# A planned single-core kernel: verdict ordered early, its branch hinted, transpositions in float32r, a corrected cost table

## The chip, the cores and the metric

The kernel runs on one core of a Trainium2 chip. The metric is device time in microseconds (us) from start to end of one execution; the figure for a kernel is the median of several executions. The engines are called as in the profile: PE (matmuls) and PEld (its weight loads), DVE (vector), ACT (scalar), POOL (GpSimd), SP (which issues all DMAs here). PEldq, DVEq, ACTq, POOLq and SPq are their sequencers, which run branches, semaphore instructions and register loads.

## The reference

A gated linear recurrence ("attention") over 768 steps for 4 x 8 heads of 48, and then two feed-forward stages on 3072 tokens of 384:

```python
scale = np.minimum(mag, 0.999) / (mag + 1e-06)        # mag = |a|
for t in range(S):
    new_re = ar * S_re - ai * S_im                    # a = scaled (a_re, a_im) at t
    new_im = ar * S_im + ai * S_re
    S_re, S_im = new_re + outer(k[t], v[t]), new_im
    y[t] = q[t] @ S_re
h = x @ w_in                                          # 3072 x 384 @ 384 x 2048
x = softplus(h) @ w_out                               # back to 384
out = (((x @ w1) * (x @ w2)) @ w3) @ w_out2           # 1024 wide
```

The weights come as float64 bit patterns, two int32 words for a number.

## The kernel before, in words

**Attention.** The time axis is cut into 24 units of 128 steps (six for each of four batches). For unit `u`, `norm(u)` makes the scaled decay `a` (`s1` to `s4`: squares, a norm, a reciprocal root in logarithms on ACT, products on DVE), `scan` multiplies the decays up over two units at a time (DVE alone), `inv(u)` divides: `s3` and `s5` write q times P and k over P into the tile `qkp`, real and imaginary part, and `s6` sends `qkp` to DRAM (`pd`) and reads it back by heads into `rs`. `mm(u)` then transposes the k half of `qkp` on PE (`kt(0)`, `kt(1)`: three transpositions each, copied to `kT` by ACT), forms the scores from `rs` (`sc`), masks them on DVE (`am`), and forms the output `yp` and the new state (`stp`). The last unit of a batch needs no state and so no transposition; units 0 and 1 take a shortcut without DRAM (`pick`).

**First feed-forward** (blocks "A"): nine blocks of tokens. `s1` multiplies with `w_in`, softplus runs on ACT and DVE, `s2a` multiplies with `w_out`. The first two blocks are in float32; the other seven split each operand into a high and a low float32r part and use three products. They run beside the attention of later tokens.

**Second feed-forward** (blocks "B"): six blocks of 512 tokens, `s3` (two products `pa`, `pb`, multiplied on DVE, split on ACT and DVE) and `s2b` with w3 and w_out2, which `early()` has multiplied together at the start (`wpa`).

**Verdict.** The fast path holds for ordinary inputs only. `check` collects minima and maxima of all weights (80 pieces, during blocks B), and at the end of the program comparisons are drawn together to one number `oki` in SBUF: DVE reduces to one column `okp`, PE transposes it to a row `okt`, DVE reduces that to `oki`. Each engine loads `oki` into a register (`values_load`) and compares; if the verdict is 0 a slow path, `general`, runs. It stands in the program between the branch and the end, so with a verdict of 1 every engine jumps over it.

**What sets the order.** All instructions of the fast path are recorded by `Plan.add` with a cost from the table `Plan.cost` and their dependencies. `Plan.flush` lays them out on the engines by list scheduling, back and forth, 16 rounds with one fixed seed, takes the best by its own costs, and emits them in that order; each engine then runs its own queue in order. The costs set nothing but the order. Nearly every instruction is issued from one line of `Plan.add` (L211 in the profile), so instructions are told apart by their tiles. Tiles with the same tag share buffers (`qkp` has one buffer; `n2` has one), and an instruction that writes a buffer waits for the readers of the tile that was there.

```python
order = sorted((k for k in start if self.ops[k][0]), key=lambda k: (start[k], k))
with self.tc.manual_schedule():
    for k in order:
        for call in self.ops[k][1]:
            call()
```

Of the kernel before, what the change touches and what calls it, by code (L numbers as in the profile page):

```python
# [66 lines left out]

VH = 64
# [11 lines left out]
class Plan:  # L80
# [57 lines left out]
    def cost(self, eng, op, outs, ins):  # L138
        n = max(self.free_size(x) for x in (*outs, *ins))
        if eng == "SP":  # L140
            size = 2 if outs[0].dtype == I16 else 4
            for _, n in outs[0].ap:
                size *= n
            rate = 270 if hasattr(ins[0].tensor, "tag_meta") else RATE
            cost = max(650 if n < 512 and self.on_chip(ins[0]) else 475, size / rate)
            if not self.on_chip(outs[0]):
                land = 5200
            elif self.on_chip(ins[0]):
                land = 2300
            elif hasattr(ins[0].tensor, "tag_meta"):  # L150
                land = 6800
            else:
                land = 2500 + size / rate
            return cost, max(land - cost, 0)
        if eng == "PE":
            n = self.free_size(outs[0])
            if op == "transpose":
                return 109, 250
# [3 lines left out]
            return ((0.75 * n + 24) / (2 if m <= 32 else 1) if m <= 64 else max(n, m) / 0.6 + 5), 250  # L162
# [3 lines left out]
        if eng == "ACT":  # L166
            return 105 + 0.88 * n, 200
# [155 lines left out]
    def flush(self):  # L323
# [26 lines left out]
        with self.tc.manual_schedule():  # L350
            for k in order:
                for call in self.ops[k][1]:
                    call()
# [13 lines left out]
def fused(ctx: ExitStack, tc: tile.TileContext, a_in, qk_in, v_in, wio, w12, w3t, wo2, q, k, v, a_re, a_im, outT):  # L367
# [38 lines left out]
    nc.vector.tensor_scalar(out=mask, in0=mask, scalar1=whenf, scalar2=None, op0=ALU.is_ge)  # L406
# [3 lines left out]
    nc.gpsimd.memset(eps_p, 1e-18)  # L410
    m2max = cp.tile([P, NCH], F32, name="m2max")
# [57 lines left out]
    def norm(u):  # L469
# [20 lines left out]
        def s3():  # L490
# [3 lines left out]
            A.activation(out=gt(n[:, 1]), in_=w, func=AF.Copy, scale=5e-7, bias=1.0)  # L494
            A.activation(out=gt(n[:, 0]), in_=w, func=AF.Copy, scale=-0.4995)

        def s4():
            n = s["nt"]
            V.scalar_tensor_tensor(
                out=n[:, 0], in0=n[:, 0], scalar=1.0, in1=n[:, 1], op0=ALU.min, op1=ALU.mult  # L500
# [131 lines left out]
    def inv(u):  # L632
# [55 lines left out]

        if u < PICK:
            return [s1, s2, s3, lambda: pick(0), s4, s5, lambda: pick(1)]  # L690
        return [s1, s2, s3, s4, s5, s6]

    def mm(u):
# [142 lines left out]
    wtop = [wp.tile([P, 2 * DM], I32, tag=tag, name=f"wtop_{tag}") for tag in ("ws", f"wa{FA - 1}")]  # L836
    for x in wtop:
        GP.memset(x, 0)

# [278 lines left out]
    for i, n in enumerate(("min", "max")):  # L1118
        bst[n] = lims[:, i * NCK : (i + 1) * NCK]
    b_x(0)  # L1120
    it = 0
    nit = (NBB - 1) * FB
    for bi in range(NBB):
        gq = {}
        for f in range(FB):
# [13 lines left out]
    for i, n in enumerate(("min", "max")):  # L1139
        V.tensor_reduce(  # L1140
            out=wlim[:, i : i + 1], in_=bst[n], axis=mybir.AxisListType.X, op=getattr(ALU, n)
        )
    okp = ap.tile([P, DM], F32, tag="v", bufs=VB, name="okp")
    c0 = 0
    for src, lim, op in (
        (pend.rearrange("p b g -> p (b g)"), 1e-3, ALU.is_ge),
        (m2max, 1e15, ALU.is_le),
        (wlim[:, 0:1], 2.0**-28, ALU.is_ge),
        (wlim[:, 1:2], 2.0**32, ALU.is_lt),
    ):  # L1150
        n = src.shape[1]
        V.tensor_scalar(out=okp[:, c0 : c0 + n], in0=src, scalar1=lim, scalar2=None, op0=op)
        c0 += n
    ok1 = okp[:, DM - 1 : DM]
    V.tensor_reduce(out=ok1, in_=okp[:, 0:c0], axis=mybir.AxisListType.X, op=ALU.min)
    okt = pst("s1", S1B, [P, NB], "okt")[0:1, 0:P]
    PE.transpose(okt, ok1, ident)
    V.tensor_reduce(out=oki, in_=okt, axis=mybir.AxisListType.X, op=ALU.min)
# [245 lines left out]
```

## Time and profile before

| | |
|---|---|
| median of 3 executions | 920.21 us (919.09 to 921.62) |
| the profiled execution, its own time | 920.99 us |
| its span, first to last instruction | 919.1 us |
| PE busy | 883.7 us, 96% of the span |
| DVE, ACT, POOL busy | 706.2, 517.2, 9.9 us |
| granted TensorE clock, mean | 0.996 of full speed |
| DMA moved | 139.16 MB, 151 GB/s |

PE's busy time joins overlapping matmuls, whose ends are modelled: it shows where PE had something to do, and not how fast. How fast is read from pieces of the chain of waits, where a run of n like matmuls stands with its length. Times inside the span count from its start. The 1.9 us between the span and the execution's own time lie outside it.

### The profile page before, as it was taken

To read this page: it belongs to the slowest core of one execution; us is meant where nothing else is said; L and a number is where in the kernel's file an instruction comes from. 1 tells how busy PE (TensorE), PEld (TensorE's weight loads), DVE (VectorE), ACT (ScalarE), POOL (GpSimd) and SP (SyncE) were. 2 spreads that over 40 slices of the span, in tenths; PEclk is the share of its full clock that TensorE was granted. 3 is DMA by queue.
4 is the path that set the end of the run, shared out by engine and by line. 5 is a ranking of instruction groups with operands and counts; after the bars stand their busy time and mean duration, and the time that the engine had idled before them with its cause. 6 is when DMAs were issued, how large, how long until landed. Compare 5 with 4: busy or idle time off the path is not lost.

```text
span 919.1 us, 18336 instructions
## 1 busy us (share of the span) xinstructions
PE 883.7 (96%) x7177; PEld 794.3 (86%) x7177; DVE 706.2 (77%) x1739; ACT 517.2 (56%) x1056; POOL 9.9 (1%) x31
## 2 busy tenths in 40 slices
PE   3998899999999999999999999999999999999995
PEld 2577788898999999999999999998888888888884
DVE  6999999999999999898997563689878885232211
ACT  6688985777678685767775655772222222131212
POOL 4000000000000000000000000000000000000000
PEclk9999999999999999999999999999999999999998
DMA  9898736445465644544454361357788773000001
GB/s 338 315 369 309 183 114 143 130 118 137 121 177 139 170 109 121 142 116 132 124 133 124 98 165 63 104 147 245 239 275 244 260 230 109 0 35 1 35 1 39
DMA packets 81361, 139.16 MB, mean 151 GB/s; under 512 B 5872, under 2 KB 49776, under 8 KB 81264
## 3 DMA queue, kind: packets, MB, share of 16 engines
q1 hardware_dynamic: 81264, 137.89, 50.3%
q8 instruction: 58, 0.95, 0.5%
q14 instruction: 39, 0.32, 0.1%
HBM read 109.56 MB, written 28.31 MB: 150 GB/s over the span
## 4 chain that ended last, share of the span: by engine, by line
PE 78%; DVE 9%; DMA 6%; ACT 2%; issue 2%; SPq 1%; ACTq 0%; DVEq 0%
PE acc L211 29%; PE s L211 18%; PE pb L211 11%; PE pa L211 11%; PE yp L211 3%; PE sc L211 3%; DMA a<-a_in 3%; DVE P L211 2%; PE wpa L211 2%; DMA wr<-wio 2%; DVE tm L211 2%; SPq L211 1%; PE stp L211 1%; PE ktp L211 1%; DMA wpd<-wpe 1%
## 5 line engine op out<-in xcount | busy, mean ns | idle before, releaser
L211 ACT ACTIVATE e<-e 128x384 f32<-128x384 f32 (+2 forms) x288 | 134.5, 486 | 2.9
L211 DVE TENSOR_TENSOR bg<-pa,bg 128x512 f32<-128x512 f32 x48 | 33.1, 691 | 97.4 <-PE pa L211 81.8
L211 DVE TENSOR_TENSOR tm<-P 128x768 f32<-128x768 f32 (+4 forms) x240 | 101.0, 438 | 1.2
L211 ACT ACTIVATE e<-s 128x384 f32<-128x384 f32 (+2 forms) x144 | 64.9, 452 | 60.4 <-PE s L211 59.2
L211 DVE SCALAR_TENSOR_TENSOR e<-s,e 128x384 f32<-128x384 f32 (+2 forms) x144 | 72.6, 508 | 23.9 <-ACT e L211 23.6
L211 ACT CAST bgg<-bg 128x512 fp32r<-128x512 f32 x48 | 29.8, 621 | 98.1 <-DVE bg L211 98.1
L211 ACT COPY bg<-pb 128x512 f32<-128x512 f32 x48 | 28.2, 588 | 96.8 <-PE pb L211 84.3
L211 DVE TENSOR_TENSOR P<-tm 128x96 f32<-128x96 f32 (+9 forms) x328 | 76.2, 271 | 1.6
L211 ACT CAST gh<-e 128x384 fp32r<-128x384 f32 x112 | 56.8, 509 | 21.9 <-DVE e L211 21.8
L211 DVE TENSOR_TENSOR gl<-e,gh 128x384 fp32r<-128x384 f32 x112 | 61.7, 552 | 9.3 <-ACT gh L211 8.8
L211 PE MATMUL wpa<-wo,w 128*128 128x384 f32 x128 | 44.5, 505 | 14.1 <-DVE w L211 14.1
L211 PE MATMUL sc<-rs 112*128 112x128 f32 x384 | 53.6, 275 | 1.1 <-DVE e L211 1.1
L211 PEld LDWEIGHTS sc<-rs 112*128 112x128 f32 x384 | 51.6, 191 | 2.3 <-DVE e L211 1.5
L211 PEld LDWEIGHTS wpa<-wo,w 128*128 128x128 f32 x128 | 24.8, 198 | 30.8 <-DVE w L211 14.3
L211 PE MATMUL acc<-bgg,bwp0h 128*128 128x512 f32 x144 | 50.8, 389 | 0.0
L211 DVE CUSTOM_DVE_ANT_0 ck<-ckr 128x384 f32<-128x384 f32 x80 | 43.4, 543 | 9.2 <-DMA ckr<-wio 3.1
L211 PE MATMUL acc<-bgg,bwp2h 128*128 128x512 f32 x144 | 49.0, 389 | 0.0
L211 DVE TENSOR_TENSOR bgg<-bg,bgg 128x512 fp32r<-128x512 f32 x48 | 33.0, 688 | 15.7 <-ACT bgg L211 15.7
L211 DVE TENSOR_REDUCE lims<-ck 128x1 f32<-128x384 f32 x80 | 43.1, 538 | 2.3
L211 PE MATMUL s<-x,w 128*128 128x128 f32 (+1 forms) x192 | 38.0, 332 | 3.0 <-DVE E L211 0.9
L211 DVE TENSOR_TENSOR am<-sc,mask 128x512 f32<-128x512 f32 x48 | 32.9, 686 | 7.9 <-PE sc L211 7.8
L211 PE MATMUL acc<-e,w 128*128 128x128 f32 (+1 forms) x192 | 37.4, 329 | 1.1 <-issue 1.1
(385 smaller groups left out, 2325.0 us busy)
## 6 DMA issues: line engine op xcount, KB each, us to landing
pd<-qkp SPq DMA_DIRECT2D x22, 768.0 KB, 3.9
rs<-pd SPq DMA_DIRECT2D x44, 384.0 KB, 6.2
ckr<-wio SPq DMA_DIRECT2D x32, 384.0 KB, 3.7
wr<-wio SPq DMA_DIRECT2D x32, 383.8 KB, 6.9
a<-a_in SPq DMA_DIRECT2D x24, 384.0 KB, 4.8
qk<-qk_in SPq DMA_DIRECT2D x24, 384.0 KB, 3.4
v<-v_in SPq DMA_DIRECT2D x24, 256.0 KB, 4.4
w12r<-w SPq DMA_DIRECT2D x16, 384.0 KB, 3.4
```

Source lines behind the costliest of these rows:

```text
L211: getattr(engine.unit, op)(*args, **kw)
```

## The change

1. **Verdict early.** The comparisons, the transposition `okt` and the reduction `oki` are recorded when the fifth block B has been recorded, not after the sixth, with a dummy operation of 30000 behind them, so that the planner sees them as a chain of 30 us that must end in time. The register load loses its run-time bounds check.
2. **Hint.** The emitted program is cut at a third of the planned time. There each of PE, ACT, DVE and SP gets one instruction more, a branch prefetch hint that names the branch over `general`. POOL gets none.
3. **Transpositions.** Units 2 to 22 but the last of a batch (18 units) copy the k half of `qkp` by a DMA (SBUF to SBUF, 384 KB) into a float32r tile `kx`, which takes the buffer of `n2`. Their transpositions (6 for a unit, 108 in all) read `kx` in float32r with a float32r identity, which ACT copies once.
4. **Norm.** The second of two ACT copies in `s3` goes (24 in all); DVE's instruction in `s4` takes its place with other constants.
5. **Mask and fills.** The comparison that makes the mask goes from DVE to POOL; two fills of POOL come earlier.
6. **Cost table.** Float32r transpositions, narrow matmuls, DMAs within SBUF and ACT on bfloat16 get other costs. So the whole order is planned anew.

```diff
@@ cost
-                land = 2300
+                land = 2200 + size / rate
...
-                return 109, 250
+                return (82 if ins[0].dtype == F32R else 109), 250
...
-            return ((0.75 * n + 24) / (2 if m <= 32 else 1) if m <= 64 else max(n, m) / 0.6 + 5), 250
+            return ((0.75 * n + 8) / 2 if m <= 32 else 0.75 * n + 24 if m <= 64 else max(n, m) / 0.6 + 5), 250
...
-            return 105 + 0.88 * n, 200
+            return 105 + (1.25 if any(x.dtype == BF16 for x in ins) else 0.88) * n, 200
@@ flush
-        with self.tc.manual_schedule():
-            for k in order:
-                for call in self.ops[k][1]:
-                    call()
+        cut = next(i for i, k in enumerate(order) if start[k] > 0.33 * best[0])
+        for part in (order[:cut], order[cut:]):
+            with self.tc.manual_schedule():
+                for k in part:
+                    for call in self.ops[k][1]:
+                        call()
+            if part[0] == order[0]:
+                self.tc.no_sync_barrier()
+                self.tc.mark_branch_hint_location("general", engines=ENGINES)
@@ fused
-    nc.vector.tensor_scalar(out=mask, in0=mask, scalar1=whenf, scalar2=None, op0=ALU.is_ge)
+    nc.gpsimd.tensor_scalar(out=mask, in0=mask, scalar1=whenf, scalar2=None, op0=ALU.is_ge)
@@ norm
-            A.activation(out=gt(n[:, 1]), in_=w, func=AF.Copy, scale=5e-7, bias=1.0)
-            A.activation(out=gt(n[:, 0]), in_=w, func=AF.Copy, scale=-0.4995)
+            A.activation(out=gt(n[:, 1]), in_=w, func=AF.Copy, scale=-0.4995 * 5e-7, bias=-0.4995)
...
-                out=n[:, 0], in0=n[:, 0], scalar=1.0, in1=n[:, 1], op0=ALU.min, op1=ALU.mult
+                out=gt(n[:, 0]), in0=half(u)[:, 0], scalar=-1.0 / 0.4995, in1=gt(n[:, 1]), op0=ALU.max, op1=ALU.mult
@@ inv
+        def s7():
+            if u % CPB < CPB - 1:
+                s["kx"] = ap.tile([P, 2, G, T], F32R, tag="n2", name=f"kx{u}")
+                SP.dma_start(s["kx"].bitcast(F32), s["qkp"][:, :, :, 1])
...
+    identr = cp.tile([P, P], F32R, name="identr")
+    A.copy(identr, ident)
@@ mm, kt
-                    PE.transpose(pt[:, g], s["qkp"][:, ri, g, 1], ident)
+                    if "kx" in s:
+                        PE.transpose(pt[:, g].bitcast(F32R), s["kx"][:, ri, g], identr)
+                    else:
+                        PE.transpose(pt[:, g], s["qkp"][:, ri, g, 1], ident)
@@ end
+    def verdict():
...
+        PE.transpose(okt, ok1, ident)
+        V.tensor_reduce(out=oki, in_=okt, axis=mybir.AxisListType.X, op=ALU.min)
+        plan.push(None, None, {len(plan.ops) - 1}, 30000, 0)
...
+            if it == nit:
+                verdict()
...
-    ok = nc.values_load(oki[0:1, 0:1], min_val=0, max_val=1)
-    with tc.If(ok < 1):
+    ok = nc.values_load(
+        oki[0:1, 0:1], min_val=0, max_val=1, skip_runtime_bounds_check_because="the least of comparisons is 0 or 1"
+    )
+    with tc.If(ok < 1, label="general"):
```

How the order moves, at three places. The end of DVE's queue before (`bgg_5_7` is the last product's low part, `oki` the verdict; L1161 and L1162 are the register load and the branch):

```order
L211 TENSOR_TENSOR bgg_5_6_1794<-bg_5_6_1793,bgg_5_6_1794 128x512
L211 TENSOR_TENSOR bg_5_7_1797<-pa5_7_1795,bg_5_7_1797 128x512
L211 TENSOR_TENSOR bgg_5_7_1798<-bg_5_7_1797,bgg_5_7_1798 128x512
L211 TENSOR_REDUCE oki_134<-okt_1803 1x1
L1161 TENSOR_LOAD oki_134
L1162 COMPARE_AND_BRANCH
```

and now, first where `oki` went, then the end:

```order
L212 TENSOR_TENSOR bgg_4_7_1777<-bg_4_7_1776,bgg_4_7_1777 128x512
L212 TENSOR_REDUCE oki_138<-okt_1783 1x1
L212 TENSOR_TENSOR bg_5_0_1789<-pa5_0_1787,bg_5_0_1789 128x512
```

```order
L212 TENSOR_TENSOR bg_5_7_1820<-pa5_7_1818,bg_5_7_1820 128x512
L212 TENSOR_TENSOR bgg_5_7_1821<-bg_5_7_1820,bgg_5_7_1821 128x512
L1182 TENSOR_LOAD oki_138
L1185 COMPARE_AND_BRANCH
```

`oki` now stands ahead of the first product of the sixth block B, and PE's last instruction before its register load is a matmul of `acc`, no longer `okt`.

SP's queue at unit 9 before (`pd` is the store of `qkp`, `rs` the reload by heads; `qk`, `v`, `a` load later units, `x2d` stores a block A):

```order
L211 DMA pd9_74<-qkp9_615 128x6x256
L211 DMA qk10_642<-qk_in 128x768
L211 DMA rs1_143<-pd9_74 48x8x256 x2
L211 DMA x2d1_58<-xoa2_0_644 128x384
L211 DMA v9_617<-v_in 128x512
L211 DMA a13_595<-a_in 128x768
```

and now:

```order
L212 DMA qk10_652<-qk_in 128x768
L212 DMA pd9_74<-qkp9_622 128x6x256
L212 DMA kx9_650<-qkp9_622 128x6x128
L212 DMA rs1_147<-pd9_74 48x8x256 x2
L212 DMA x2d1_58<-xoa2_0_654 128x384
L212 DMA v9_626<-v_in 128x512
```

The new copy `kx` stands right behind the store and ahead of the reload, as in 15 of the 18 units; in units 2, 4 and 6 it stands ahead of the store.

PE's queue at the transpositions of unit 9 before (`sc` are the scores, which need `rs`; `s1_3_..` and `acc` are a block A):

```order
L211 MATMUL acc_515<-gl_2_14_632,ww14h_627 128x384
L211 MATMUL ktp9_1_660<-ident_114,qkp9_615 128x128 x2
L211 MATMUL ktp9_0_652<-ident_114,qkp9_615 128x128
L211 MATMUL sc9_0_662<-rs1_143 128x128 x4
L211 MATMUL acc_515<-gh_2_15_639,ww14h_627 128x384
L211 MATMUL acc_515<-gh_2_15_639,ww15l_636 128x384
```

and now:

```order
L212 MATMUL acc_522<-gh_2_15_648,ww15l_645 128x384
L212 MATMUL ktp9_0_663<-identr_156,kx9_650 128x128
L212 MATMUL s1_3_2_673<-xh3_543,ww2h_514 128x384
L212 MATMUL acc_522<-gl_2_15_649,ww14h_635 128x384
L212 MATMUL s1_3_2_673<-xh3_543,ww2h_514 128x384 x2
L212 MATMUL s1_3_2_673<-xh3_543,ww2l_515 128x384
L212 MATMUL ktp9_0_663<-identr_156,kx9_650 128x128 x2
L212 MATMUL ktp9_1_670<-identr_156,kx9_650 128x128 x3
```

The transpositions read the copy and still stand ahead of the scores, mixed with matmuls of a block A.

## Rows read from the trace of the kernel before

**Rows 1.** The page's busy us, share of the span and instructions of the engines.

```profile
PE 883.7 (96%) x7177; PEld 794.3 (86%) x7177; DVE 706.2 (77%) x1739; ACT 517.2 (56%) x1056; POOL 9.9 (1%) x31
```

**Rows 2.** Stages: from:to, length; busy us of PE, PEld, DVE, ACT, POOL; clock, DMA.

```profile
core 0: us, PE busy (x) PEld busy (x) DVE busy (x) ACT busy (x) POOL busy (x), PEclk, DMA share, GB/s
...
14.10:75.00 60.90, 59.28 (x364) 39.58 (x364) 59.97 (x152) 44.41 (x69) 0.00 (x0) 1.00 0.94 347
75.00:180.00 105.00, 97.43 (x1154) 87.65 (x1155) 102.20 (x274) 82.92 (x200) 0.00 (x0) 1.00 0.58 169
180.00:540.00 360.00, 358.20 (x3765) 350.30 (x3764) 324.55 (x851) 253.85 (x552) 0.00 (x0) 1.00 0.50 131
...
620.00:909.90 289.90, 289.84 (x1280) 239.71 (x1278) 161.39 (x359) 74.10 (x120) 0.00 (x0) 1.00 0.42 134
```

**Rows 3.** The chain that ended last, its end: start, us, what.

```profile
903.84 5.91 PE acc L211 x26
...
909.77 0.59 ACT xob L211
```

**Rows 4.** The register load, L1161: duration min/median/max ns, first and last start us.

```profile
L1161 SPq TENSOR_LOAD <-oki x1: 557/557/557, 910.8 to 910.8; - x1
L1161 SPq FUSED_REGOPS  x1: 186/186/186, 911.4 to 911.4; - x1
```

**Rows 5.** The branch, L1162, and the first instructions behind it; columns as above.

```profile
L1162 SPq EVENT_SEMAPHORE  x8: 17/17/17, 915.1 to 915.6; - x8
...
L1162 PEldq COMPARE_BRANCH  x1: 3608/3608/3608, 910.9 to 910.9; - x1
...
L1162 SPq COMPARE_BRANCH  x1: 50/50/50, 911.7 to 911.7; - x1
...
L1162 DVEq EVENT_SEMAPHORE  x1: 21/21/21, 914.8 to 914.8; - x1
```

**Rows 6.** The program's last line, L1399; columns as above.

```profile
L1399 POOLq EVENT_SEMAPHORE  x4: 17/17/17, 918.4 to 919.0; - x4
...
L1399 SPq DRAIN  x3: 7/7/13, 916.2 to 918.6; - x3
...
L1399 DVEq DRAIN  x2: 10/72/135, 918.2 to 918.7; - x2
```

**Rows 7.** DVE in order of time, its last product: start, us.

```profile
905.32 0.69 DVE L211 TENSOR_TENSOR bgg<-bg,bgg 128x512 fp32r<-128x512 f32 x1 [0.69 <-ACT bgg L211]
```

**Rows 8.** The stores of the output: from issue to landing.

```profile
DMA to landing us min/median/max: 2.0/2.7/4.8
```

**Rows 9.** The chain of waits, runs of like matmuls: start, us, what.

```profile
300.15 0.66 PE ktp L211 x6
```

```profile
388.84 4.51 PE s L211 x26
...
718.88 2.49 PE pb L211 x11
```

**Rows 10.** DMA issues: KB each, median us from issue to landing.

```profile
pd<-qkp SPq DMA_DIRECT2D x22, 768.0 KB, 3.9
rs<-pd SPq DMA_DIRECT2D x44, 384.0 KB, 6.2
...
qk<-qk_in SPq DMA_DIRECT2D x24, 384.0 KB, 3.4
```

**Rows 11.** In order of time: the start of PE's first product; ACT copies of the norm.

```profile
11.93 1.05 ACT L211 CAST wtop_wa<-w3r 128x768 f16<-128x768 bf16 x1 [0.41 <-DMA w3r<-w3t]
...
13.10 0.95 DVE L211 SCALAR_TENSOR_TENSOR w<-w3r,wtop_wa 128x768 int32<-128x768 int32 x1
```

```profile
L211 ACT ACTIVATE nt<-P 128x384 f32<-128x384 f32 x48 | 23.0, 517 | 8.9 <-DVE P L211 8.8
```

**Rows 12.** DMA queues that fetch instructions: packets, MB, share of 16 engines.

```profile
q8 instruction: 58, 0.95, 0.5%
q14 instruction: 39, 0.32, 0.1%
```

More of the change, by code (lines that the diff above doesn't have):

```diff
@@ L66 @@
 NBB = NT // NX
+ENGINES = [getattr(mybir.EngineType, n) for n in ("PE", "Activation", "DVE", "SP")]
 VH = 64
@@ L410, in fused @@
     nc.gpsimd.memset(eps_p, 1e-18)
+    wtop = [wp.tile([P, 2 * DM], I32, tag=tag, name=f"wtop_{tag}") for tag in ("ws", f"wa{FA - 1}")]
+    for x in wtop:
+        nc.gpsimd.memset(x, 0)
     m2max = cp.tile([P, NCH], F32, name="m2max")
@@ L687, in s6 @@
                 )
+        def s7():
+            if u % CPB < CPB - 1:
+                s["kx"] = ap.tile([P, 2, G, T], F32R, tag="n2", name=f"kx{u}")
+                SP.dma_start(s["kx"].bitcast(F32), s["qkp"][:, :, :, 1])
         if u < PICK:
             return [s1, s2, s3, lambda: pick(0), s4, s5, lambda: pick(1)]
-        return [s1, s2, s3, s4, s5, s6]
+        return [s1, s2, s3, s4, s5, s6, s7]
+    identr = cp.tile([P, P], F32R, name="identr")
+    A.copy(identr, ident)
     def mm(u):
@@ L835, in fused @@
     w32 = [None] * FA
-    wtop = [wp.tile([P, 2 * DM], I32, tag=tag, name=f"wtop_{tag}") for tag in ("ws", f"wa{FA - 1}")]
-    for x in wtop:
-        GP.memset(x, 0)
     def shifted(dst, src):
@@ L1119, in fused @@
         bst[n] = lims[:, i * NCK : (i + 1) * NCK]
+    def verdict():
+        for i, n in enumerate(("min", "max")):
+            V.tensor_reduce(
+                out=wlim[:, i : i + 1], in_=bst[n], axis=mybir.AxisListType.X, op=getattr(ALU, n)
+            )
+        okp = ap.tile([P, DM], F32, tag="v", bufs=VB, name="okp")
+        c0 = 0
+        for src, lim, op in (
+            (pend.rearrange("p b g -> p (b g)"), 1e-3, ALU.is_ge),
+            (m2max, 1e15, ALU.is_le),
+            (wlim[:, 0:1], 2.0**-28, ALU.is_ge),
+            (wlim[:, 1:2], 2.0**32, ALU.is_lt),
+        ):
+            n = src.shape[1]
+            V.tensor_scalar(out=okp[:, c0 : c0 + n], in0=src, scalar1=lim, scalar2=None, op0=op)
+            c0 += n
+        ok1 = okp[:, DM - 1 : DM]
+        V.tensor_reduce(out=ok1, in_=okp[:, 0:c0], axis=mybir.AxisListType.X, op=ALU.min)
+        okt = pst("s1", S1B, [P, NB], "okt")[0:1, 0:P]
+        PE.transpose(okt, ok1, ident)
+        V.tensor_reduce(out=oki, in_=okt, axis=mybir.AxisListType.X, op=ALU.min)
+        plan.push(None, None, {len(plan.ops) - 1}, 30000, 0)
     b_x(0)
@@ L1135, in fused @@
                 check(r, ap.tile([P, DM], F32, tag="v", bufs=VB, name=f"ck{ncheck[0]}"))
+            if it == nit:
+                verdict()
         s2b(FB - 1, gq.pop(FB - 1))
         evac(NX, lambda i: outT[i * P : (i + 1) * P, bi * NX : (bi + 1) * NX], f"b{bi}", b_room)
[L1139 to L1158, printed above, removed]
     plan.flush()
     fast.close()
-    ok = nc.values_load(oki[0:1, 0:1], min_val=0, max_val=1)
-    with tc.If(ok < 1):
+    ok = nc.values_load(
+        oki[0:1, 0:1], min_val=0, max_val=1, skip_runtime_bounds_check_because="the least of comparisons is 0 or 1"
+    )
+    with tc.If(ok < 1, label="general"):
         general(tc, q, k, v, a_re, a_im, wio, w12, w3t, wo2, xg, gws, outT)
```

## The prediction

> **What bounds the kernel now.** I read the page first: PE is busy 883.7 us of 919.1 [rows 1]. Then the stages, to see where that holds [rows 2]. From 180 to 540 us PE lacks 1.8 of 360 us, and from 620 us to its last matmul 0.06 of 289.9: there only less work for PE helps. From 14.1 to 75 us DVE is busy 59.97 of 60.90 us, and from 75 to 180 us 102.20 of 105, while PE lacks 7.6: in this stretch DVE sets the pace, and PE's gaps are its shadow. Third, the end of the chain of waits [rows 3]: a run of 26 matmuls ends at 909.75, ACT's last copy at 910.36, and then come 8.8 us in which no engine computes. That tail is the place to look at, by the sequencers' rows [rows 4 to 6].
>
> The reader is to see this in them. SP loads the verdict at 910.8 (0.56 us), does a run-time check from 911.4, and branches at 911.7. Behind every branch stands a hole: the next instruction of SP comes at 915.1, that of DVE (which branched with PE at 910.9) at 914.8, and PE's branch itself is shown with 3.6 us. All of them jump over the slow path. DVE then has a second hole, from 914.8 to its DRAIN at 918.2. SP needs 1.1 us for 16 semaphore instructions and is at its DRAIN at 916.2. DVE's DRAIN is the last thing waited for; POOL's semaphore instructions follow from 918.4 to 919.0, and the span ends 0.9 us after that DRAIN.
>
> **The change, part by part**, against the profiled execution: 919.1 of span and 1.9 around it, 920.99, which is 0.8 above the median of 920.21.
>
> *Tail.* With the verdict early, DVE has nothing behind its last product, which ends at 906.0 [rows 7]. It loads and branches near 906.7; both holes together (3.9 and 3.4) end at 914.0 and no longer count. `okt` on PE stood behind the last matmul, so PE's last matmul comes no earlier for its going. ACT's copy still ends at 910.36, and the last store still goes out at 910.4, so SP is last. Its load stays at 910.8 to 911.3; without the check (from FUSED_REGOPS at 911.4 to the branch at 911.7) it branches at 911.4. If the hint works, it goes on at 911.5 and, by the 1.1 us of 16 instructions, is done at 912.6. It must also see the last store land: issued at 910.4 and at least 2.0 on its way [rows 8], 912.4, and up to 0.6 us of instructions stand behind that wait: 913.0. Add the 0.9: the span ends between 913.5 and 913.9. Gain 5.2 to 5.6, I take **5.4**. POOL has no hint, but gets the verdict tens of us earlier and has its hole in peace. The hint itself is one instruction on four queues; the trace has none, and I price it at nothing to 0.2 us on PE by the sequencers' rows of 0.02 to 0.19 us, and take 0.1.
>
> Whether the hint works no row shows. What a jump costs, the rows do show: 3.4 to 3.9 us [rows 5]. The Trainium skill speaks against it ("Runtime: NRT & Kernel Launch", section on instruction fetch mechanics): it says that an engine holds two blocks of code and that "Prefetch is purely sequential", so that a taken branch to a target outside them waits for its block. By that rule a hint given some 600 us ahead keeps nothing, and the sum would have the tail of the first rival below. The holes behind the branches agree with the rule. The block size that the page gives (16 KiB) fits queue q8 here (0.95 MB in 58 packets) and not q14 (0.32 MB in 39, 8 KB) [rows 12].
>
> *Transpositions.* Six in float32 take 0.66 us in the chain, 0.110 each [rows 9]. A float32r transposition of 128 columns is in no row. Float32r matmuls take 0.1735 with 384 columns (4.51 us for 26) and 0.2264 with 512 (2.49 for 11) [rows 9], so 0.053 for 128 columns more, and a straight line gives 0.068 at 128: a gain of 0.042. That is one end. The other is no gain, if a load of the weights and not the columns sets the pace, since each transposition brings its own. The straight line is far from its rows, so I take the middle, 0.089, a gain of 0.021. Of 108, the units 2, 3, 4 and 6 have 24, which lie before 180 us by the planned place, where DVE sets the pace; 84 lie where PE is full. 84 x 0.021 = 1.8, and I count the 24 half (0.2): **2.0**; ends 0 and 4.5.
>
> *The copy `kx`.* 18 DMAs of 384 KB add 7 MB to a stretch with DMA engines half busy [rows 2], and each is an issue on SP ahead of the reload `rs`. A load of the same size lands after 3.4 us, the store ahead of it takes 3.9 [rows 10], so `kx` lands some 4 to 5 us after the store's issue, while `rs` needs the store's landing and 6.2 more: 10 us. `sc` needs `rs` and stands behind the transpositions on PE, only some matmuls of a block A behind them in the place shown. So I cost it at nothing; the cover is `sc`'s own wait. If that is gone, PE stands in its queue (second rival). The delay of `rs` by one issue is covered likewise. `kx` also holds the buffer of `n2` until the transpositions are done, so the next unit's squares wait for PE; units come every 20 us or so between 180 and 540 (17 in 360 us), and the chain through `kx` is some 10.
>
> *Copies, mask, start.* 24 ACT copies at 0.5 us [rows 11] go: 11 us of an engine that is busy 254 of 360 us, nothing on the path. The mask leaves DVE ahead of PE's first product and of both stretches above. That product hangs on ACT's cast, which waits for a DMA (11.93) and on DVE behind it (13.10) [rows 11]; that DMA is in the same place of SP's queue. Nothing.
>
> *New order.* Every instruction may move. The gaps to be won or lost are those of 75 to 180 us, 7.6; elsewhere there are hardly any. DVE's work there is the same, so I forecast the same gaps, give or take 3.
>
> Sum: -5.4 + 0.1 - 2.0 = -7.3, that is 913.7 for the execution and, taken off the median, 920.21 - 7.3 = **912.9**.
>
> **The rivals.** *The hint does nothing.* Then SP's hole stays: branch at 911.4, next instruction 3.4 later at 914.8, 1.1 and 0.9 more: 916.8, a gain of 2.3 instead of 5.4. With -2.0 the time is 916.0. For it: no row shows a hint, and it is given two thirds of the program ahead. Against: the instruction names the branch that it is for, so it need not hold the code until then. By the page's rule on prefetch above, this would be the case. Chance 0.14.
>
> *PE waits for `kx`* (the other side). PE runs its queue in order; if a copy lands late, everything behind the transpositions waits. The place is each of 18 units, the price what is missing each time; from 0.41 us a unit it eats the 7.3, and with 0.8 it is 14.4, giving 912.9 + 14.4 = 927.3, or 920.0 at 0.4. For it: the store of 768 KB goes first through the same engines, and the trace has stores that take 3.9. Against: the reload comes some 5 us later than the copy, and `sc`, close behind the transpositions, waits for that already. Chance 0.06.
>
> *The new order loses gaps.* The plan is made anew with other costs, and 75 to 180 us has the room for it: 3 to 5 us of gaps more take the place of what the transpositions give: 912.9 + 4 = 916.9. Against: DVE, not the order on PE, sets that stretch. Chance 0.10. The forecast has 0.70.
>
> **How the numbers follow.** A measurement of this kernel can tell some 0.3% from no change, 2.8 us: faster is below 917.4, slower above 923.0. The forecast gives 0.69 faster and 0.01 same; the first rival, at 916.0 give or take 2, 0.11 and 0.03; the third 0.06 and 0.04; the second 0.01 same and 0.05 slower. Sum: 0.86, 0.09, 0.05. The range: down to transpositions at 0.068 (2.5 more) and gaps 3 fewer, 907.5; up over the first rival, and most of the third, to 918.0.
>
> **What would show it.** Right: the rows of the branch have the next instructions of PE, ACT, DVE and SP within 0.3 us behind it, SP's DRAIN 2 to 3 us after the last store's issue, the span ending some 4 us after ACT's last copy begins; transpositions of 0.07 to 0.09 in the chain, a run of 6 below 0.55. Wrong: holes of 3.4 behind SP's branch (first rival); waits of PE at `ktp` for the DMA `kx` among the longest (second); PE busy less than 97 of 105 us from 75 to 180 (third).

## The result, and the profile after

The changed kernel takes 909.97 us (median of 4 runs, 908.70 to 911.78), beside 919.89 for the kernel before on the same chip: a ratio of 0.9899, 95% interval 0.9885 to 0.9912. Forecast were 912.9, in a range of 907.5 to 918.0. So the direction and the range held, and the time fell by 2.6 us more than the sum on record says. Behind that stand two errors of opposite sign, a tail that gained less and gaps that shrank by 5.5 us. Times are medians over all executions of a kernel; the ratios leave out the few in a slow state, such as one of 1485.55 us with seed 211, without which its median below is 915.21.

The profiled execution has a span of 907.2 us (909.05 with what lies around it). The page's row of busy time, which answers to [rows 1]:

```profile
PE 882.0 (97%) x7177; PEld 793.0 (87%) x7177; DVE 702.1 (77%) x1738; ACT 511.4 (56%) x1033; POOL 12.0 (1%) x32
```

The stages, to be laid beside [rows 2] (columns as there):

```profile
14.10:75.00 60.90, 60.90 (x438) 41.59 (x439) 59.97 (x155) 43.73 (x68) 0.00 (x0) 1.00 0.93 340
75.00:180.00 105.00, 99.07 (x1103) 89.68 (x1102) 104.18 (x283) 83.26 (x200) 0.00 (x0) 1.00 0.68 195
180.00:540.00 360.00, 359.50 (x3900) 352.20 (x3899) 323.45 (x844) 251.71 (x540) 0.00 (x0) 1.00 0.56 147
540.00:620.00 80.00, 80.00 (x501) 77.27 (x502) 54.46 (x100) 52.13 (x101) 0.00 (x0) 1.00 0.45 128
620.00:902.50 282.50, 282.33 (x1242) 232.09 (x1240) 153.84 (x347) 71.11 (x114) 0.00 (x0) 1.00 0.43 132
```

From 75 to 180 us PE is now busy 99.07 of 105 us, where it was 97.43, and DVE 104.18, where it was 102.20: in the stretch that DVE paces, DVE itself waits less. From 14.1 to 75 us PE has no gap left (1.6 us before), from 180 to 540 it lacks 0.5 us (1.8 before), and from 540 to 620 it lacks nothing, where the kernel before lacked 1.1:

```profile
540.00:620.00 80.00, 78.94 (x620) 77.07 (x619) 50.48 (x95) 52.15 (x105) 0.00 (x0) 1.00 0.43 119
```

So the gaps fell by 1.6 us in the stretch from 75 to 180 us and by 3.9 us in the three others.

The page's busy time and the trace's first and last matmul give an account of the whole difference of 11.9 us in span; PE's gaps are the time between these two matmuls less its busy time:

| us | before | after | difference |
|---|---|---|---|
| PE's first matmul | 14.10 | 13.93 | -0.2 |
| PE busy | 883.69 | 881.96 | -1.7 |
| PE's gaps | 12.05 | 6.56 | -5.5 |
| end of PE's last matmul to the end of the span | 9.28 | 4.80 | -4.5 |

These are two executions. The medians differ by 9.9 us and not by 11.9: the profiled execution of the kernel before was 1.1 us above its median of 919.89, that of the changed kernel 0.9 below its own. In which rows these 2 us stand can't be told.

The last row is told by the sequencers. The register load, L1182, the branch and what follows it, L1185, and the program's last line, L1422 (duration ns min/median/max, first and last start us), which answer to [rows 4 to 6]:

```profile
L1182 SPq TENSOR_LOAD <-oki x1: 548/548/548, 903.5 to 903.5; - x1
```

```profile
L1185 SPq EVENT_SEMAPHORE  x8: 17/17/17, 905.3 to 905.9; - x8
L1185 POOLq COMPARE_BRANCH  x1: 45/45/45, 852.7 to 852.7; - x1
L1185 DVEq COMPARE_BRANCH  x1: 84/84/84, 899.1 to 899.1; - x1
L1185 DVEq EVENT_SEMAPHORE  x1: 21/21/21, 899.7 to 899.7; - x1
L1185 PEldq COMPARE_BRANCH  x1: 403/403/403, 899.9 to 899.9; - x1
...
L1185 ACTq COMPARE_BRANCH  x1: 68/68/68, 903.3 to 903.3; - x1
L1185 ACTq EVENT_SEMAPHORE  x1: 17/17/17, 903.8 to 903.8; - x1
L1185 SPq COMPARE_BRANCH  x1: 70/70/70, 904.2 to 904.2; - x1
```

```profile
L1422 POOLq DRAIN  x3: 34/82/113, 855.6 to 907.0; - x3
L1422 SPq DRAIN  x3: 7/7/13, 906.4 to 906.8; - x3
L1422 DVEq DRAIN  x2: 10/14/17, 899.9 to 906.8; - x2
...
L1422 PEldq BRANCH_PREFETCH_HINT  x1: 45/45/45, 293.3 to 293.3; - x1
L1422 SPq BRANCH_PREFETCH_HINT  x1: 60/60/60, 293.4 to 293.4; - x1
```

And the last store of the output, its issue and its landing:

```profile
L212 SPq DMA_DIRECT2D outT<-xob x1: 332/332/332, 903.2 to 903.2; - x1
...
DMA to landing us min/median/max: 2.2/2.2/2.2
```

The hint stands at 293 to 296 us on each of four queues and takes 45 to 60 ns. DVE goes on 0.6 us after its branch, ACT 0.5, PE's branch is shown with 0.4, where the rows of before had 3.4 to 3.9 [rows 5]. POOL, which has no hint, still has its hole (852.7 to 855.6), in peace. SP's next instruction comes 1.2 us after its branch, at 905.3, when the last store has landed (903.2 and 2.2): it waits for that store, and 0.5 us of it are the branch's own, as the last experiment shows.

### The profile page after: what moved, and what is told of

It is laid out like the page before. It is cut to its first block, busy times and chain, and to the rows that moved or that the text cites. A ratio compares the mean times of both kernels' runs of the same rounds, so it can differ in the third digit from the quotient of the medians.

```text
span 907.2 us, 18398 instructions
## 1 busy us (share of the span) xinstructions
PE 882.0 (97%) x7177; PEld 793.0 (87%) x7177; DVE 702.1 (77%) x1738; ACT 511.4 (56%) x1033; POOL 12.0 (1%) x32
## 5 line engine op out<-in xcount | busy, mean ns | idle before, releaser
L212 DVE TENSOR_TENSOR gl<-e,gh 128x384 fp32r<-128x384 f32 x112 | 62.0, 556 | 10.2 <-ACT gh L212 9.8
L212 DVE TENSOR_TENSOR bgg<-bg,bgg 128x512 fp32r<-128x512 f32 x48 | 33.1, 689 | 16.9 <-ACT bgg L212 16.9
```

The source lines that it names most:

```text
L212: getattr(engine.unit, op)(*args, **kw)
```

## The experiments

The account left one question and three prices. What made the gaps fall by 5.5 us, when the forecast left them alone "give or take 3"? Theory A: the corrected table of costs gives the planner a better order. Theory B: each plan of this kernel draws its gaps by chance. Theory C: the copy `kx` (DVE's waits before it rewrites `qkp` fell from 3.8 us, for PE's transpositions, to 0.6, for the copy) or the shorter chain of the norm. The prices are those of the hint, the early verdict and the transpositions. The kernel before was timed again beside each set of runs, with medians from 918.9 to 920.2 us, and the ratios are to these.

### The hint alone

```diff
             if part[0] == order[0]:
                 self.tc.no_sync_barrier()
-                self.tc.mark_branch_hint_location("general", engines=ENGINES)
...
-    with tc.If(ok < 1, label="general"):
+    with tc.If(ok < 1):
```

> The changed kernel with the hint taken out and nothing else (the program stays cut in two at the same place, with the same order on every engine). Time of the changed kernel: 909.97 us; of the kernel before: 919.89. Theory H, the hint fetches the code of the branch target: SP's hole behind its branch returns, from 1.17 us (in the changed kernel mostly the landing of the last store, 2.2 us after its issue) to some 3.4 to 3.9 as in the kernel before; the 16 semaphore instructions (1.1 us) then follow with no wait, since the store has landed: the end comes 2.2 to 2.7 us later, 912.2 to 912.7; DVE shows its second hole again, off the path; PE's gaps stay near 6.6 us. Rival N, the hint does nothing and the short hole comes from the shape of the branch (its label, no run-time check ahead of it): no change, 909.7 to 910.3, with SP's hole still near 1.2.

Measured: 911.63 us, ratio 0.9917 (0.9903 to 0.9931), 0.6 us below the range of theory H and above that of rival N. The branch's line in this run:

```profile
L1184 SPq EVENT_SEMAPHORE  x8: 17/17/17, 908.5 to 909.0; - x8
...
L1184 DVEq COMPARE_BRANCH  x1: 72/72/72, 899.9 to 899.9; - x1
L1184 PEldq COMPARE_BRANCH  x1: 3492/3492/3492, 900.7 to 900.7; - x1
L1184 DVEq EVENT_SEMAPHORE  x1: 21/21/21, 902.8 to 902.8; - x1
L1184 ACTq COMPARE_BRANCH  x1: 50/50/50, 904.1 to 904.1; - x1
...
L1184 SPq COMPARE_BRANCH  x1: 50/50/50, 904.9 to 904.9; - x1
L1184 ACTq EVENT_SEMAPHORE  x1: 17/17/17, 907.5 to 907.5; - x1
```

The holes are back: ACT's is 3.4 us (904.1 to 907.5), DVE's 2.9, PE's branch is 3.5 again; rival N falls. DVE's second hole, which theory H expected, is not: its DRAIN follows at 902.9. The tail behind PE's last matmul is 7.17 us, 2.4 longer than with the hint, as much as theory H has it, but SP's row does not show it in the way that theory H has it. SP goes on 3.6 us after its branch (904.9 to 908.5), and its first instruction waits for the last store. Theory H took that store to have landed by then; it was issued at 903.9 and took 4.5 us, so it landed at 908.45, and the span ends 1.94 us later, exactly as long after the landing as in the changed kernel. So in this run the hole of SP and the late landing end together and can't be told apart. That SP has a hole of its own without the hint is seen in [rows 5], where the store had landed at 912.5 and SP went on at 915.1. The DMA queues in the 1.4 us from this store's issue (packets, MB, share; then KB and us to landing) show instructions being fetched beside it:

```profile
q8 instruction: 1, 0.02, 9.2%
...
outT<-xob SPq DMA_DIRECT2D x1, 256.0 KB, 4.5
```

That packet of 16 KB starts at 904.92, as SP branches, and lasts 2.05 us; the last section comes back to it.

The medians differ by 1.7, less than the tails; executions of one order differ by two or three microseconds. One reason stands in this run's waits of PE:

```profile
PE ktp L212 <- DMA kx<-qkp: 1.4, 1, 1.4
```

The order is that of the changed kernel, whose profiled execution has no such wait: one copy of 18 came late by 1.4 us, near 110 us.

### The old table in the changed kernel, the new table in the kernel before

In the changed kernel the four lines were put back, in the kernel before they were put in:

```diff
-                land = 2200 + size / rate
+                land = 2300
...
-                return (82 if ins[0].dtype == F32R else 109), 250
+                return 109, 250
...
-            return ((0.75 * n + 8) / 2 if m <= 32 else 0.75 * n + 24 if m <= 64 else max(n, m) / 0.6 + 5), 250
+            return ((0.75 * n + 24) / (2 if m <= 32 else 1) if m <= 64 else max(n, m) / 0.6 + 5), 250
...
-            return 105 + (1.25 if any(x.dtype == BF16 for x in ins) else 0.88) * n, 200
+            return 105 + 0.88 * n, 200
```

> The changed kernel, planned with the old table of costs (four lines); the same instructions, another order. What is open: PE's idle time between matmuls fell from 12.05 us to 6.56 in the profiled executions, 5.5 us that the prediction had not counted. Theory A, the corrected table gives an order that fits the chip better: the gaps return to 10 to 13 us, and the time rises by 3 to 6 us, to 913 to 916, with PE busy in 75 to 180 us back at some 97.5 of 105. Rival B, any new plan draws its gaps by chance: gaps anywhere from 6 to 13 us, and the time by as much, not told apart from A by this run alone. Rival C, the copy kx and the copy less in the norm's chain shorten what PE waits for, whatever the order: gaps stay within 1 us of 6.6 and the time at 909 to 911.

> The kernel before, planned with the corrected table of costs and nothing else of the change: the same instructions, another order. Its own tail, 9.3 us behind PE's last matmul, and its PE work, 883.7 us, stay; only PE's idle time between matmuls (12.05 us in the profiled execution) can move. Theory A, the table brought the fall of the gaps: they come to 6 to 8 us and the time to 914 to 916. Theory B, each new plan draws its gaps by chance, the table only being one way to draw again (the changed kernel with the verdict late, which has the table, had 10.94): gaps between 7 and 14 us, with no side preferred, time 915 to 922.

Measured: the changed kernel with the old table 914.06 (ratio 0.9944, 0.9931 to 0.9956), gaps 9.16 us; the kernel before with the new table 918.04 (0.9975, 0.9959 to 0.9991), gaps 10.34. In both pairs the new table has the fewer gaps, by 2.6 and 1.7. In the first run A's time came in, and PE's 97.5 us from 75 to 180 (97.58), but not its gaps of 10 to 13; in the second neither its gaps nor its time. B allows all of it. Both of these profiled executions also have 3.4 us at half the clock, which gaps do not count. C falls by the first: same instructions, and the gaps are up by 2.6. A part for the table is not excluded by these two runs.

### No copy `kx`

```diff
-        return [s1, s2, s3, s4, s5, s6, s7]
+        return [s1, s2, s3, s4, s5, s6]
```

> The changed kernel without the 18 copies kx: the 108 transpositions are float32 again, straight from the buffer qkp (the plan follows, at 109 ns for each). Theory T, float32r saves 0.025 us a transposition (84 ns from start to start against 109): PE's busy time rises by 2 to 2.7 us and so does the time, to 912.0 to 912.7, with the gaps still near 6.6 us. Rival C, the copy also brought the fall of the gaps, since DVE need not wait for PE's transpositions before it writes the next unit into qkp (that wait was 3.8 us before and 0.6 after): the gaps rise to 9 to 12 us, and the time to 914 to 917. Rival B, chance of the new plan: gaps 6 to 13 with no row that names qkp.

Measured: 914.13 us, ratio 0.9953 (0.9938 to 0.9967), runs from 911.3 to 916.6; PE busy 882.79, gaps 9.08 in the profiled execution, which was the fastest of the six. PE's work rose by only 0.8 us and the gaps by 2.5, in a new order. DVE's wait for the transpositions ahead of `qkp` is back (3.0 us), so this alone would agree with C; but draws below that keep the copy have gaps as large. Since the order moved with the edit, the run separates little, and the transpositions were priced again below with the order held.

### The verdict late, the hint kept

```diff
-        plan.push(None, None, {len(plan.ops) - 1}, 30000, 0)
...
-            if it == nit:
-                verdict()
...
+    verdict()
     plan.flush()
```

> The changed kernel with the verdict ordered at the end, as in the kernel before (its place in the program and the node of 30 us that pulls it ahead are undone); the hint stays. With the hint the branch costs SP no hole of its own, so: theory E, the early verdict is worth what stands between the last verdict instruction and the branch on the path: DVE's last reduction would come after PE's last matmul (the transposition okt stands near the end of PE's queue), SP loads the verdict after that, as it did at 910.8 us of the kernel before, about the time at which it issues the last store. So at most 0.5 us: 909.7 to 910.5. Rival L, without the early verdict the engines other than SP (DVE and POOL, which has no hint) branch so late that their holes and DRAINs end last: POOL's hole of 2.9 us and its semaphore instructions come after SP's, and the time rises by 1.5 to 3 us, to 911.5 to 913.

Measured: 915.18 us, ratio 0.9960 (0.9947 to 0.9972), above both ranges: tail 5.79 us (4.80 with the early verdict) and gaps 10.94 (6.56). The gaps are a new draw again: an edit that touches the end moved the order from 75 to 180 us as well (PE busy 95.59 of 105). The tail is rival L's mechanism at a smaller size, in these rows of the branch and the last line:

```profile
L1183 POOLq COMPARE_BRANCH  x1: 45/45/45, 907.3 to 907.3; - x1
```

```profile
L1420 SPq DRAIN  x3: 7/7/13, 910.0 to 911.6; - x3
L1420 POOLq DRAIN  x3: 34/82/113, 911.2 to 911.8; - x3
```

POOL has no hint. It branches at 907.3, has its 3.9 us of hole and comes to its DRAIN at 911.2, some 1.1 us after SP was through (its first two DRAINs stand at 910.0 and 910.1). Given the hint, the early verdict is worth about this 1 us in the tail.

### Other draws of the same plan

One number was changed, the seed of the noise in the planner's second round:

```diff
-SEED = 214
+SEED = 215
```

> The changed kernel with 215 for the seed of the planner's noise in place of 214: the same instructions, table, hint and verdict, another order. Theory A, the table makes the order fit the chip, so any plan by it is good: gaps 5.5 to 8 us, time 909 to 911.5. Theory B, chance, with a plan picked well in the changed kernel: gaps 8 to 12 us, all of the rise between 75 and 260 us, time 911.5 to 916, more if the granted clock falls for some microseconds behind a gap, as in the run with the old table (0.5 for 3.4 us, worth 1.7).

> The changed kernel with seed 216: a second draw. Theory A: gaps 5.5 to 8 us, time 909 to 911.5, and within 1 us of the draw with 215. Theory B: gaps 8 to 12, time 911.5 to 916, and the two draws differ by 1 to 4 us.

> The kernel before with seed 215: a draw by the old table. Theory A, the old table makes a poor order whatever the seed: gaps 11 to 14 us, time 918.5 to 921. Theory B: gaps between 7 and 14, time 914 to 922.

> The changed kernel with seed 211, a third draw. The draws so far: seeds 214, 215, 216 gave gaps of 6.6, 9.2 and 11.8 us and times of 910.0, 914.6 and 918.1. Theory B, chance, the changed kernel's own plan being picked well: gaps 7.5 to 12, time 911.5 to 918. Theory A, with 216 an outlier: gaps 6 to 8, time 909 to 912.

Measured, with the two kernels of the change for comparison (gaps and PE busy of the profiled execution; "half clock" is the time between PE's first and last matmul in which the granted clock was 0.5, that is 1.2 GHz and not 2.4; these three columns are of that one execution):

| kernel | seed | gaps us | half clock us | PE busy us | time us | ratio to before |
|---|---|---|---|---|---|---|
| changed | 214 | 6.56 | 0 | 881.96 | 909.97 | 0.9899 (0.9885 to 0.9912) |
| changed | 215 | 9.19 | 3.4 | 884.09 | 914.55 | 0.9947 (0.9931 to 0.9962) |
| changed | 211 | 10.71 | 6.8 | 884.77 | 915.74 | 0.9954 (0.9938 to 0.9969) |
| changed | 216 | 11.81 | 10.2 | 887.35 | 918.08 | 0.9983 (0.9968 to 0.9997) |
| before | 214 | 12.05 | 0 | 883.69 | 919.89 | 1 |
| before | 215 | 8.67 | 3.4 | 884.08 | 917.28 | 0.9979 (0.9968 to 0.9989) |

The same instructions, the same table, hint and verdict take 910 to 918 us. Theory A falls (its 5.5 to 8 us of gaps came in none of three draws), the old table's as well (8.67 and not 11 to 14), and B stands, with one miss: seed 216 is slower than its 916. The spread is the order's: four profiled executions that share the changed kernel's order (above and below) have gaps of 6.4 to 7.5 us. The change's own plan is the best drawn here, and the spread of 8 us is more than any part of the change is worth. A gap can cost more than itself: the stages of the draw with 216, where PE pauses:

```profile
core 0: us, PE busy (x) PEld busy (x) DVE busy (x) ACT busy (x) POOL busy (x), PEclk, DMA share, GB/s
77.00:79.00 2.00, 1.50 (x13) 1.31 (x12) 2.00 (x9) 2.00 (x7) 0.00 (x0) 1.00 0.95 324
79.00:81.00 2.00, 0.31 (x2) 0.31 (x3) 2.00 (x8) 1.24 (x5) 0.00 (x0) 1.00 1.00 392
81.00:83.00 2.00, 2.00 (x15) 2.00 (x14) 1.96 (x5) 2.00 (x8) 0.00 (x0) 0.70 1.05 413
83.00:85.00 2.00, 1.39 (x7) 1.09 (x6) 2.00 (x7) 1.83 (x6) 0.00 (x0) 0.50 1.02 408
85.00:88.00 3.00, 3.00 (x16) 3.00 (x15) 3.00 (x6) 2.66 (x8) 0.00 (x0) 0.50 1.04 418
```

PE is idle 1.69 of the 2 us from 79 to 81, and from 81.8 its clock is at half. Half of the 10.2 us at that clock is 5.1 us of work done late; PE's busy time is 5.4 above that of the changed kernel. How much of this an execution has varies: over the twelve with seed 216 the time goes from 915.33 us, at a mean granted clock of 0.998, to 922.70, at 0.992.

### The transpositions, with the order held

The copy stays, the plan is told the same costs, and only the type of the 108 transpositions goes back:

```diff
-                return (82 if ins[0].dtype == F32R else 109), 250
+                return (82 if "kx" in ins[0].tensor.name else 109), 250
...
-                s["kx"] = ap.tile([P, 2, G, T], F32R, tag="n2", name=f"kx{u}")
-                SP.dma_start(s["kx"].bitcast(F32), s["qkp"][:, :, :, 1])
+                s["kx"] = ap.tile([P, 2, G, T], F32, tag="n2", name=f"kx{u}")
+                SP.dma_start(s["kx"], s["qkp"][:, :, :, 1])
...
-                        PE.transpose(pt[:, g].bitcast(F32R), s["kx"][:, ri, g], identr)
+                        PE.transpose(pt[:, g], s["kx"][:, ri, g], identr.bitcast(F32))
```

> The changed kernel with the 108 transpositions in float32 again, still from the copy kx, and planned as if they were float32r, so that every instruction of every engine keeps its place. This prices the transpositions with the order held still, as the runs with other orders could not. Theory T, 25 ns each where PE is full (84 against 109 from start to start), 84 of 108 counted: 2.1 us; PE's busy time 883.5 to 884.7 against 881.96, gaps near 6.6, time 1.5 to 2.7 above the changed kernel's 909.97: 911.5 to 912.7. Rival S, the float32r transposition is shorter by itself but the weight load of the next one (0.14 us) or the matmul behind it takes the difference back: busy within 0.7 us of 881.96, time 909.5 to 910.7.

Measured: 911.43 us, ratio 0.9923 (0.9911 to 0.9936); PE busy 883.52, gaps 6.39. PE's work is up by 1.56 us (1.6 to 1.9 against the three profiles with the changed kernel's order): theory T, at its lower end. The time is up by 1.5 in the medians and by 2.1 between the profiled executions; 0.8 of the latter is the last store, which landed after 2.9 us and not after 2.2. So PE's work is the price, and the time agrees with it only roughly. The same place in order of time, of the changed kernel and then of this run (start us, us):

```profile
383.99 0.34 PE L212 MATMUL acc<-gh,ww3l 128*128 128x384 f32 x1
384.16 0.37 PE L212 MATMUL ktp<-identr,kx 128*128 128x128 f32 x3
384.37 0.76 PE L212 MATMUL s<-xh,ww6l 128*128 128x384 f32 x3
...
387.30 0.39 PE L212 MATMUL acc<-gh,ww3l 128*128 128x384 f32 x1
```

```profile
384.96 0.34 PE L212 MATMUL acc<-gh,ww3l 128*128 128x384 f32 x1
385.14 0.49 PE L212 MATMUL ktp<-identr,kx 128*128 128x128 f32 x3
385.38 0.77 PE L212 MATMUL s<-xh,ww6l 128*128 128x384 f32 x3
...
388.36 0.42 PE L212 MATMUL acc<-gh,ww3l 128*128 128x384 f32 x1
```

From one `acc` to the other, with six transpositions among the same matmuls, PE takes 3.31 us in float32r and 3.40 in float32: 0.015 a transposition. Times 108 that is 1.6. Two transpositions in a row start 68 ns apart in float32r and 109 in float32 (medians), which would be 0.041 each; from a transposition to PE's next instruction of any kind it is 84 against 109. Among other matmuls more than half of the gain is lost, as rival S has it, but not all.

### `kx` for the late units only

```diff
-            if u % CPB < CPB - 1:
+            if u % CPB < CPB - 1 and u > 6:
                 s["kx"] = ap.tile([P, 2, G, T], F32R, tag="n2", name=f"kx{u}")
```

> The changed kernel with the copy kx and float32r only from unit 7 on; the units 2, 3, 4 and 6 are transposed in float32 from qkp (15 of the 18 copies stay or so; the plan follows). Three of the runs so far had PE wait 1.3 to 1.9 us for a kx once, mostly near 110 us, where DVE sets the pace and float32r is worth little. Theory W, that wait is a cost of the change which this takes away: no wait of PE for kx before 180 us, gaps 5 to 7, time 908.5 to 910.5, beside or below the changed kernel. Theory B, a new plan is a new draw, and that weighs more than the wait: gaps 8 to 12, time 912 to 917.

Measured, with 14 of the 18 copies left: 912.99 us, ratio 0.9933 (0.9920 to 0.9946), gaps 8.17. No wait for `kx` before 180 us, and a new order that costs more than the wait: theory B. Whether the early copies are worth keeping can't be read from it.

### The last store on the last semaphore

```diff
+            plan.halves = nm in ("b0", "b1") or (nm, i) == ("b2", 0)
             SP.dma_start(dst(i), o[:, 0:n])
+            plan.halves = False
...
+            n = args[0].shape[1] // 2 if halves else 0
+            for x in (slice(0, n), slice(n, 2 * n)) if halves else ():
+                engine.unit.dma_start(args[0][:, x], args[1][:, x])
+            if not halves:
+                getattr(engine.unit, op)(*args, **kw)
```

> The changed kernel with seven of the output stores of the last stage, long before the end, issued as two halves each; the DMAs take SP's eight semaphores in turn, so that the last store now falls on the eighth and not on the first, and every instruction of PE, DVE and ACT keeps its place. In the changed kernel the first of SP's 16 semaphore instructions waits for the last store, so all 16 (1.1 us) stand behind its landing. Theory Q, that order is what the prediction missed: seven of the first eight now run while the store is still on its way, 9 stand behind the landing (0.6 us), the tail behind PE's last matmul falls from 4.80 to 4.2 to 4.4 us for the same landing time, and the time is 909.3 to 909.7, no more than can be told from 909.97. Rival D, the hole behind SP's branch lasts as long as the landing itself, and the instructions come after it whatever they wait for: tail 4.7 to 4.9. The seven halves cost SP 7 issues in a stretch where it has time: nothing on PE.

Measured: 909.14 us (908.64 to 911.54), ratio 0.9888 (0.9869 to 0.9907). That can't be told from the changed kernel's 0.9899, as expected. The rows tell more. The branch's line, and the last store:

```profile
L1194 SPq EVENT_SEMAPHORE  x8: 17/17/17, 905.2 to 906.7; - x8
...
L1194 SPq COMPARE_BRANCH  x1: 70/70/70, 904.7 to 904.7; - x1
```

```profile
L219 SPq DMA_DIRECT2D outT<-xob x1: 332/332/332, 903.7 to 903.7; - x1
DMA to landing us min/median/max: 3.0/3.0/3.0
```

SP's first semaphore instruction now comes 0.5 us behind the branch, and the eighth at 906.7, when the store has landed; from there to SP's DRAIN (907.3) it is 0.6 us, not 1.1. So theory Q holds and rival D falls. But this store took 3.0 us to land, and the last one of the changed kernel 2.2, so the tail came out at 5.10 us, above the range that was expected for an equal landing; what follows the landing is 1.40 us, where the changed kernel has 1.94.

Two runs above say the same without the halves, since with other numbers of DMAs the last store falls on another semaphore. Without the 18 copies six of SP's eight waits stand ahead of the landing (908.05), and the first of them 0.5 us behind the branch:

```profile
L1185 SPq EVENT_SEMAPHORE  x8: 17/17/17, 907.3 to 908.1; - x8
...
L1185 SPq COMPARE_BRANCH  x1: 70/70/70, 906.8 to 906.8; - x1
```

With four copies fewer four stand ahead of it. What follows the landing is 1.47 and 1.61 us.

## Why the prediction was right, and where it was wrong

**What bounds the kernel** was read right in kind: PE's work, PE's gaps and the tail each moved the time by what it lost.

**Tail, -5.4 forecast, -4.5 measured.** The mechanism was right: the hint closes the holes, SP is last, its branch comes 1.0 us after the last store's issue, and the store lands 2.2 us after it. The term that was mis-sized is "up to 0.6 us of instructions stand behind that wait": all 16 stood there, 1.1 us, because the semaphore of the last store is the first that SP waits for. Also "the next instruction within 0.3 us" was too hopeful: with the hint it is 0.4 to 0.6. From the store's issue to the span's end the forecast had 3.1 to 3.5 us; measured were 4.1, and SP's DRAIN came 3.2 us after that issue, where the sign for being right was 2 to 3. One reading was loose: DVE's two holes, ending at 914.0, "no longer count" beside an SP that is done at 913.0 only if the hint closes them, which the same sum assumes.

**The hint.** Its price (0.1) is right. The first rival, "the hint does nothing", had the sentence of the Trainium skill for it ("Runtime: NRT & Kernel Launch", section on instruction fetch mechanics) that "Prefetch is purely sequential". The runs show otherwise here: in one and the same order ACT's hole is 3.4 us without the hint and 0.5 with a hint that was given some 610 us ahead, DVE's 2.9 and 0.6; SP's is 3.4 in the kernel before, without a hint, and 0.5 in the runs in which its first instruction does not wait for the last store. The holes without a hint agree with the same section of the Trainium skill, by which a taken branch out of the loaded blocks waits for a fetch.

**The early verdict.** The forecast put its worth into DVE's two holes. With the hint DVE has 0.6 us, late or early; what the early verdict takes off the path is POOL's hole, about 1 us.

**Transpositions, -2.0 forecast, -1.6 measured** with the order held, between the ends of 0 and 4.5. The size came out near, by a saving that is smaller in place (0.015 each) than the one assumed (0.021), over all 108 and not over 84 and a half of 24. The straight line was right by itself: 0.068 is what two in a row measure. That among other matmuls more than half of the gain is lost again no row had shown, and that the middle of the two ends came near is luck.

**`kx` at nothing, the second rival.** PE's gaps did not grow by 18 waits. But it was not nothing in every execution: of the profiles with the changed kernel's order one has a wait of 1.4 us, one shows 0.6 before a transposition, the other two none. The price is a late copy now and then, near 109 us in both, in the stretch where DMA engines are 0.68 busy against 0.56 in the next, and not something per unit.

**The new order, "the same gaps, give or take 3".** This is the step that failed: -5.5. The forecast took the gaps of 75 to 180 us for DVE's shadow and so for fixed by DVE's work. They are not: with the same work PE is busy from 95.9 to 99.8 us of that stretch, by the seed drawn, and with DVE busy 103.7 us it is 95.81 in one run (the new table in the kernel before) and 99.64 in another (no `kx`). It also held that "elsewhere there are hardly any" gaps, though [rows 2] have 1.6 us from 14.1 to 75 and 1.8 from 180 to 540; of the fall of 5.5 only 1.6 came from 75 to 180, and 3.9 from elsewhere. "Give or take 3" was too narrow as well; the plans run here have 6.4 to 12.05 us of gaps, and six of the 14 profiled executions lose clock on top, which the forecast had no term for. The third rival, an order that loses 3 to 5 us, was a matter of the seed: with 216, gaps of 11.8 and 5.1 of lost clock come to 16.9 us, where the kernel before had 12.05, and the time is 918.08. That is just outside the range, where the three other seeds are inside it; that the time came out below the forecast is the luck of the draw.

So the parts that were worked out are worth -6.1 (4.5 and 1.6) where -7.3 was forecast, and the fall of the gaps, 5.5 between the profiled executions and perhaps 2 less between the medians, came with the order. Why this order has fewer gaps than its sisters is open: table, copies and verdict each moved the order when they were undone, so that their own effect on the gaps can't be separated from the draw. Open too is what the parts would be worth in the mean over orders; three further draws of the changed kernel and one of the one before are too few for that, and the ratios of these draws (0.9947, 0.9954, 0.9983 against 0.9979) are closer than the parts' 6 us would make them.

The version with the last store on the last semaphore is as fast as the changed kernel, faster than the kernel before, and has the shorter chain behind the landing; no run here beats the changed kernel by more than can be told.

## What to carry to other kernels

Where a planner with noise sets the order, price an edit with the order held (the same costs and dependencies told to the planner), and size the draw with a few seeds before a gain of under one per cent is put down to the edit. The branch at this program's end cost a hole on most engines that meet there; a hint closed it on those that got one, and an early operand hid it on the one that did not. Then look at what is waited for first behind the last store: every semaphore instruction that could run while it lands should stand ahead of that wait.

## What the runs showed of the hardware that was not expected

- The last store, 256 KB, landed 2.0 to 2.2 us after its issue in eight of the 14 profiles, 2.9 to 3.1 in five, and 4.5 in the run without the hint. Kernels with one order fall on both sides. The DMA queues show what goes with it: in the 1.4 us from the issue a packet of instructions (q8 or q14) starts in each of the six late ones, 1.0 to 1.3 us after the issue, and in none of the eight others. The changed kernel first, then the run with float32 transpositions in the same order (packets, MB, share; KB, us to landing):

```profile
outT<-xob SPq DMA_DIRECT2D x1, 256.0 KB, 2.2
```

```profile
q14 instruction: 1, 0.01, 2.9%
...
outT<-xob SPq DMA_DIRECT2D x1, 256.0 KB, 2.9
```

That the fetch delays the store is what these rows suggest; no run was made to show it.
- A branch with a hint is not free: 0.4 to 0.6 us where the next instruction had nothing else to wait for. Without one it was 2.5 to 4.4 on SP, ACT, DVE and POOL, and on PE 3.5 and 3.6 in two runs, but none of note (0.4) in the kernel before with seed 215. One ACT with the hint took 1.2 (seed 216), for which no row gives the reason.
- The granted clock was at half for 3.4 us at a time, or 6.8, near gaps of PE: one of 2.6 us with seed 215, one of 2.2 with 216 (above). Not near each: with the verdict late a gap of 2.1 us left it at full. Each 3.4 us is by arithmetic 1.7 us of PE's work done late; PE's busy time with one such stretch was higher by 0.4 us (the kernel before) and 2.1 (the changed kernel) than with seed 214.
